# A three-stage kernel ordered by its own planner: the planner's durations, its margins and the priorities of the inverses are changed

## The chip, the cores and the metric

The kernel runs on one core of a Trainium2 chip. Five engines work beside each other, each through its own list of instructions and in the order of that list: TensorE (PE: matrix products, with PEld for loading weights), VectorE (DVE), ScalarE (ACT), GpSimd (POOL) and SyncE (SP), which here starts nearly all transfers. An instruction whose input is not there yet holds up everything behind it on its engine. The metric is the device time of one launch in microseconds (us); three runs of the kernel before gave 1203.41 us as the median, from 1199.62 to 1203.91.

## The reference

Three layers follow each other. The first is a recurrent attention with a state matrix, for 4 batches x 8 heads, 768 time steps and a head width of 48:

```python
for t in range(S):
    kt, vt, bt = (k_n[:, :, t], v[:, :, t], beta[:, :, t, None])
    y[:, :, t] = np.einsum('bhd,bhde->bhe', q[:, :, t], state)
    v_old = np.einsum('bhde,bhd->bhe', state, kt)
    state = state + bt[:, :, :, None] * np.einsum('bhd,bhe->bhde', kt, vt - v_old)
```

Its output, 3072 tokens x 384, goes through `h = x @ w_in` (384 x 2048), the curve `g` (0 up to h = -1, (h + 1)^2 / 4 up to h = 1, then h), and `g @ w_out`. The third layer scales each token by its root mean square and by `rms_g`, and computes `(silu(xn @ w_gate) * (xn @ w_val)) @ w_out` with a hidden width of 1536.

## The kernel before

**Attention.** Time is cut into 12 chunks of 64 steps. Within a chunk the recurrence becomes a triangular system, which is solved with its inverse. A unit `u` is one chunk of two batches (their 8 heads each, one batch on each half of the 128 partitions), so a chunk has two units. For units of two chunks together (`GRP`; the first two groups hold one chunk each) `inverse(g)` (L498) inverts the 32x32 triangles on POOL: 31 steps of a product `tmp` (L518) and an addition into `xi` (L524). Then ACT transposes the result into `nt` (L526), SP stores it, and for each unit POOL makes `wt` of it (`a_mz`, L545 and L546). `b_vn` (L600) scales the values in `kvb` on POOL. PE multiplies `wt` and `kvb` to `tr` (`b_tr`, L666), then `px`, `ds` and the transposed output `xps`.

**First network.** Block `j` is the 256 tokens of chunk `j`. For each of 16 slices `f` of the hidden width `m1(j, f)` (L747) does nine products into `hps`, two ACT instructions (L757, L758), a DVE maximum (L761), an ACT copy (L767) and a DVE subtraction (L769) that splits the result into two parts, and nine products into `acc`. A block ends with the root mean square (`m1_rms`, L808), whose result SP stores (L837).

**Weights.** They come as 64-bit numbers. `w_dec` (L245) loads a tile, and ACT and DVE decode it into two 32-bit parts. Tiles of the first network (`n == 1`, 32 of them) stay in SBUF; the 36 of the second (`n == 2`, DVE L280 to L285) are stored to HBM (`w2d`, L289) and loaded again later.

**Second network.** Its order is written out by hand; it begins after everything above and isn't touched by the change.

**What sets the order.** The stages of attention, weights and first network are Python generators, and `Flow` puts them in order while the program is built. A stage names its engine, a cost in us, what it needs, which buffers it takes and gives back, a priority and perhaps a `lag`. `Flow.start` (L80) reckons the earliest time at which a stage could run: its engine free, its needs done plus `lag` plus `HOP` if they come from another engine, its buffers free; a transfer (its cost is a pair) also waits for the transfers before it. `Flow.step` (L96) takes for each engine the stage that could start first (on PE: the least idle time, then the priority), and of these the earliest; it then adds the cost to the engine's reckoned time. So the order of each engine's list, which holds on the chip, comes from reckoned times. Beyond `RUSH` (45 us) a transfer is reckoned to land `LAND` after its bytes. Where PE is reckoned idle while the kernel starts, `spin` fills the gap with products nobody uses. `PG` (L842) gives the priority of each inverse group and of what prepares it; a lower number goes first.

Of the kernel before, what the change touches and what calls it, by code (L numbers as in the profile page):

```python
# [22 lines left out]
B, H, S, D = 4, 8, 768, 48  # L23
# [28 lines left out]
S = Stage  # L52


class Flow:
# [2 lines left out]

    HOP, ISSUE, FLY, LAND, RUSH = 0.4, 0.47, 0.65, 2.0, 45.0
    TILED = ("a_gram", "a_mw", "b_gs", "b_tr", "b_x", "b_ds")
    CHAIN = ("b_tr", "b_x", "b_xT")
    SWITCH, KEEP, STAY, AHEAD = 0.2, 10, 0, 0.9

    def __init__(self, **bufs):
# [13 lines left out]
    def start(self, p):  # L80
        key, st, i = p[1], p[3], p[4]
        t = self.free.get(st.eng, 0.0)
        for n in (*st.needs, (*key, i - 1)) if i else st.needs:
            if n not in self.done:
                return None
            e, x = self.done[n]
            t = max(t, x + st.lag + (0.0 if e == st.eng else self.HOP))
        if isinstance(st.cost, tuple):
            t = max(t, self.free.get("DMA", 0.0) - self.ISSUE - self.FLY - 0.7)
        for r in st.acq:  # L90
            if not self.toks[r]:
                return None
            t = max(t, self.toks[r][0] + self.HOP)
        return t

    def step(self):  # L96
        first = {}
        for p in self.live:
            st = p[3]
            if len(st.alt) > 1:  # L100
                st.eng, st.cost = min(st.alt, key=lambda a: max(self.free.get(a[0], 0.0), self.now) + a[1])
            t = self.start(p)
            if t is not None:
                e, k = p[3].eng, (t, p[0] + p[3].dp)
                if p[1][0] in self.CHAIN and p[1][1] < 2 and t < self.free.get(e, 0.0) + self.AHEAD:
                    k = (0.0, -500, t)
                elif e == "PE":
                    late = max(0.0, t - self.free["PE"] - 0.05)
                    k = (late, k[1] - ((self.KEEP if self.tiled else self.STAY) if (p[1][0] in self.TILED) == self.tiled else 0), t)
                if e not in first or k < first[e][0]:  # L110
                    first[e] = (k, p)
        if not first:
            return False
        t, p = min(((k[-1] if len(k) == 3 else k[0], p) for k, p in first.values()), key=lambda b: (b[0], b[1][0]))
        key, st, i = p[1], p[3], p[4]
        self.now, self.eng = t, st.eng
        if st.eng == "PE":
            self.idle(t - self.free["PE"])
            if (key[0] in self.TILED) != self.tiled:
                self.tiled = not self.tiled  # L120
                t += self.SWITCH
        for r in st.acq:
            self.toks[r].pop(0)
        if isinstance(st.cost, tuple):
            n, c = st.cost
            self.free[st.eng] = t + self.ISSUE * n
            end = max(self.free.get("DMA", 0.0), t + self.ISSUE + self.FLY) + c
            self.free["DMA"] = end
            end += self.LAND if t > self.RUSH else 0.9
        else:  # L130
            end = self.free[st.eng] = t + st.cost
        p[3], p[4] = next(p[2], None), i + 1
        self.done[(*key, i)] = self.done[key] = (st.eng, end)
        if p[3] is None:
            self.live.remove(p)
        else:
            del self.done[key]
        for r in st.rel:
            self.toks[r] = sorted(self.toks[r] + [end])
        return True  # L140
# [14 lines left out]
def kernel_body(  # L155
# [14 lines left out]
    stg = ctx.enter_context(tc.tile_pool(name="stg", bufs=4))  # L170
# [74 lines left out]
    def w_dec(n, f, i):  # L245
        if n == 2:
            needs = [("w_dec", 1, NF1 - 1, 1)]
        else:
            needs = [("a_gram", EARLY - 1)] if f + SK * i > 14 else []
        if n == 1:  # L250
            needs = needs + ([("inv0", 1 if f + SK * i < 9 else 19)] if f + SK * i >= 4 else [])
        me = ("w_dec", n, f, i)
        mem = "wp" if n == 1 and f + SK * i < 10 else "stg"
        yield S("SP", (1, 1.09) if n == 1 else (2, 2.18), needs, (mem,) * n)
        if mem == "wp":
            st = early([128, 2 * DM], "wst").bitcast(I64)
        else:
            st = stg.tile([128, DM], I64, name="wst", tag="wst")
        nc.sync.dma_start(out=st, in_=(w1 if n == 1 else w2)[f, :, DM * i:DM * i + DM])
        wu = st.bitcast(U32).rearrange("p (n t) -> p n t", t=2)  # L260
        wf = st.bitcast(F32).rearrange("p (n t) -> p n t", t=2)
        w0 = wu[:, :, 0]
        if n == 2:
            sv = stg.tile([128, 4 * DM], U16, name="wsv", tag="wst")
            nc.sync.dma_start(out=sv[:, 0:4 * DM - 2], in_=w2[f, :, DM * i:DM * i + DM].bitcast(U16)[:, 1:4 * DM - 1])
        yield S("ACT", 0.85, (), ("dec",))
        y = dcp.tile([128, DM], U32, name="dy", tag="dy")
        a = dac.pop(0)
        nc.scalar.activation(out=y.bitcast(F32), in_=wf[:, :, 1], func=ACTF.Copy, scale=2.0**-112)
        nc.scalar.activation(out=a.bitcast(F16).rearrange("p (n t) -> p n t", t=2)[:, :, 1], in_=wf[:, :, 1], func=ACTF.Copy, scale=2.0**-60)  # L270
        if n == 1:
            yield S("DVE", 1.5, (), ("wp",), (mem,))
            t = wp.tile([128, 2, DM], F32R, name="w", tag="w")
            yf = y
        else:
            yield S("DVE", 1.95, (), (), ("dec",))
            t = st.bitcast(F32R).rearrange("p (a b) -> p a b", a=2)
            yf = t[:, 0, :].bitcast(U32)
        hi, lo = t[:, 0, :], t[:, 1, :]
        nc.vector.scalar_tensor_tensor(out=yf, in0=y, scalar=3, in1=a, op0=ALU.logical_shift_left, op1=ALU.bitwise_or)  # L280
        nc.vector.tensor_scalar(out=a, in0=yf, scalar1=0xFF800000, scalar2=None, op0=ALU.bitwise_and)
        if n == 2:
            v = sv.bitcast(U32).rearrange("p (n t) -> p n t", t=2)[:, :, 0]
            nc.vector.tensor_scalar(out=v, in0=v, scalar1=0x1FFFFFF, scalar2=None, op0=ALU.bitwise_and)
            nc.vector.scalar_tensor_tensor(out=lo, in0=v, scalar=2.0**-36, in1=a.bitcast(F32), op0=ALU.mult, op1=ALU.mult)  # L285
            dac.append(a)
            yield S("SP", (1, 1.09), (), (), ("stg", "stg"))
            w2d[f, i] = dram.tile([128, 2, DM], F32, name=f"w2d{f}_{i}", tag=f"w2d{f}_{i}")
            nc.sync.dma_start(out=w2d[f, i], in_=t.bitcast(F32))  # L289
            return  # L290
        nc.vector.scalar_tensor_tensor(out=lo, in0=w0, scalar=2.0**-52, in1=a.bitcast(F32), op0=ALU.mult, op1=ALU.mult)
        dac.append(a)
        yield S("ACT", 0.41)
        nc.scalar.activation(out=hi, in_=y.bitcast(F32), func=ACTF.Copy)
        pre = f + SK * i <= PRE
        bank = "ea" if pre else "at"
        yield S("PE", 1.0, (), (bank,), ("dec",))
        if pre:
            fl.pre += 1
            ps = accp.tile([128, 512], F32, name="wlo", tag=f"acc{fl.pre % 2}")[:, 0:DM]  # L300
        else:
            ps = ap_.tile([128, DM], F32, name="wlo", tag="at")
        nc.tensor.matmul(out=ps, lhsT=ident, rhs=y.bitcast(F32), start=True, stop=False)
        nc.tensor.matmul(out=ps, lhsT=ineg_r, rhs=hi, start=False, stop=False)
        nc.tensor.matmul(out=ps, lhsT=ident_r, rhs=lo, start=False, stop=True)
        yield S("ACT", 0.45, (), (), (bank,), alt=[("DVE", 0.58)])
        if fl.eng == "ACT":
            nc.scalar.activation(out=lo, in_=ps, func=ACTF.Copy)
        else:
            nc.vector.tensor_copy(lo, ps)  # L310
        w1t[f, i] = t
# [433 lines left out]
    x2 = {}  # L745
# [62 lines left out]
    def m1_rms(j):  # L808
        yield S("ACT", 0.9, [("m1", j, NF1 - 1)], ("s",))
        t = x2[j]  # L810
# [22 lines left out]
        yield S("DVE", 1.3, (), (), ("w_",))  # L833
        for k in range(KD):
            nc.vector.scalar_tensor_tensor(out=t[:, k, :], in0=t[:, k, :], scalar=rg[:, k:k + 1], in1=ri, op0=ALU.mult, op1=ALU.mult)
        yield S("SP", (1, 1.09), (), (), ("x2",))
        nc.sync.dma_start(out=xn_d[j], in_=x2.pop(j))  # L837


    SK = 3  # L840
    PRE = 8
    PG = (-100, -50, -20, -10, 20, 50, 80)  # L842
    NW2 = 18
    fl = Flow(
        at=4, h=2, wp=34, stg=4, dec=ND, kk=2, ka=1, al=2, inv=1, tx=2, wt=2, z=2, kt=2, kvb=2, xs=2, xt=2,
# [14 lines left out]
    with tc.manual_schedule():  # L860
# [8 lines left out]
        fl.idle = spin  # L869
        fl.add(PG[0] + 6, inv0)  # L870
        for g, us in enumerate(GRP):
# [204 lines left out]
```

## Time and profile before

| | |
|---|---|
| median of 3 runs | 1203.41 us |
| the profiled execution's own time | 1204.66 us |
| its span | 1202.8 us |
| PE busy | 1119.7 us (93%) |
| DVE, ACT, POOL busy | 672.1, 576.2, 282.9 us |

The span runs from the first to the last instruction; the execution's own time is 1.9 us longer. Busy time is an average over parts with different limits, so the profile is read by stretches: the attention and the first network together last until about 748 us, the second network from there to the end. "Idle before" an instruction and what ended it say who waited for whom. The granted clock is the share of TensorE's full clock in a stretch.

### The profile page before, as it was taken

How to read it: one execution, taken by the hardware profiler on the slowest of the kernel's cores; microseconds unless marked ns; L12 is line 12 of the kernel's file. 1: busy time of each engine (PE TensorE's matmuls, PEld its weight loads, DVE VectorE, ACT ScalarE, POOL GpSimd, SP SyncE). 2: the span in 40 equal slices, each digit the busy share in tenths (PEclk: the TensorE clock that was granted, in tenths of full speed). 3: DMA queues.
4: the chain of work that ended last, by engine and by line, in shares of the span. 5: the costliest groups of instructions: out<-in, count | busy, mean ns of one | idle time of the engine just before them, and what ended most of it. 6: DMA issues, size and time to landing. Idle time of an engine off the chain costs nothing.

```text
span 1202.8 us, 27917 instructions
## 1 busy us (share of the span) xinstructions
PE 1119.7 (93%) x11526; PEld 1021.9 (85%) x11526; DVE 672.1 (56%) x1373; ACT 576.2 (48%) x1385; POOL 282.9 (24%) x479
## 2 busy tenths in 40 slices
PE   7877896897998999799999999999999999999998
PEld 6665686886998998799999999999888888888887
DVE  7968876867576768556465555543333333333333
ACT  4787765565856585555656566432222212122212
POOL 3283848557177108400100000000000000000000
PEclk9998998998988999899999999999999999999999
DMA  7986589584876585413212076010101001010000
GB/s 216 286 240 157 158 213 286 138 229 135 247 227 155 190 249 191 101 33 94 63 33 76 2 277 249 14 32 10 31 10 35 18 1 53 1 44 10 20 7 26
DMA packets 165902, 137.02 MB, mean 114 GB/s; under 512 B 115088, under 2 KB 127632, under 8 KB 165776
## 3 DMA queue, kind: packets, MB, share of 16 engines
q1 hardware_dynamic: 164960, 135.20, 37.8%
q8 instruction: 90, 1.47, 0.5%
q14 instruction: 36, 0.29, 0.1%
q10 hardware_dynamic: 816, 0.05, 0.0%
HBM read 100.88 MB, written 34.34 MB: 112 GB/s over the span
## 4 chain that ended last, share of the span: by engine, by line
PE 64%; POOL 15%; DVE 6%; DMA 5%; issue 4%; SPq 3%; ACT 3%; POOLq 0%; DVEq 0%; ACTq 0%
PE gv L725 8%; PE gv L724 8%; PE gv L726 8%; POOL xi L524 8%; PE acc L724 8%; PE acc L725 8%; PE acc L726 7%; POOL tmp L518 7%; PE hps L724 4%; PE hps L725 3%; PE hps L726 3%; SPq L509 2%; PE gs L611 2%; DMA nt<-scr_a 2%; DMA wst<-in_w 2%
## 5 line engine op out<-in xcount | busy, mean ns | idle before, releaser
L724 PE MATMUL acc<-g,w 128*128 128x256 f32 x648 | 190.5, 294 | 12.6 <-DVE x L806 6.9
L725 PE MATMUL acc<-g,w 128*128 128x256 f32 x648 | 187.0, 289 | 5.1 <-DVE g L769 5.1
L726 PE MATMUL acc<-g,w 128*128 128x256 f32 x648 | 185.8, 287 | 0.0
L724 PE MATMUL hps<-xh,w 128*128 128x256 f32 x576 | 168.1, 292 | 18.4 <-DVE w__4404 L761 6.1
L740 ACT ACTIVATE xh<-fix 128x512 fp32r<-128x512 f32 x60 | 37.9, 632 | 281.6 <-PE acc L726 275.7
L741 DVE TENSOR_TENSOR xl<-fix,xh 128x512 fp32r<-128x512 f32 x60 | 41.6, 694 | 228.9 <-ACT xh L740 228.9
L725 PE MATMUL hps<-xl,w 128*128 128x256 f32 x576 | 165.5, 287 | 0.0
L726 PE MATMUL hps<-xh,w 128*128 128x256 f32 x576 | 165.2, 287 | 0.0
L724 PE MATMUL gv<-fix,w 128*128 128x512 f32 x360 | 140.1, 389 | 0.0
L725 PE MATMUL gv<-fix,w 128*128 128x512 f32 x360 | 140.1, 389 | 0.0
L726 PE MATMUL gv<-fix,w 128*128 128x512 f32 x360 | 140.0, 389 | 0.0
L724 PEld LDWEIGHTS acc<-g,w 128*128 128x128 f32 x648 | 126.4, 195 | 15.4 <-DVE x L806 7.2
L725 PEld LDWEIGHTS acc<-g,w 128*128 128x128 f32 x648 | 126.7, 195 | 7.2 <-DVE g L769 7.0
L724 PEld LDWEIGHTS hps<-xh,w 128*128 128x128 f32 x576 | 113.0, 196 | 21.4 <-DVE w__4404 L761 6.4
L757 ACT ACTIVATE s<-hps 128x256 f32<-128x256 f32 x192 | 73.4, 382 | 111.8 <-PE hps L726 102.8
L726 PEld LDWEIGHTS acc<-g,w 128*128 128x128 f32 x648 | 126.6, 195 | 0.0
L518 POOL TENSOR_TENSOR tmp<-nt,xi 128x87 f32<-128x87 f32 (+21 forms) x186 | 102.4, 550 | 77.7 <-DMA nt<-scr_a 63.6
L524 POOL TENSOR_TENSOR xi<-xi,tmp 128x87 f32<-128x87 f32 (+21 forms) x186 | 111.0, 597 | 14.6
L725 PEld LDWEIGHTS hps<-xl,w 128*128 128x128 f32 x576 | 112.9, 196 | 0.0
L726 PEld LDWEIGHTS hps<-xh,w 128*128 128x128 f32 x576 | 112.8, 196 | 0.0
L758 ACT ACTIVATE s<-s,vhalf 128x256 f32<-128x256 f32 x192 | 97.9, 510 | 6.2
L726 PEld LDWEIGHTS gv<-fix,w 128*128 128x128 f32 x360 | 67.6, 188 | 14.1
(758 smaller groups left out, 2304.5 us busy)
## 6 DMA issues: line engine op xcount, KB each, us to landing
wst<-in_w SPq DMA_DIRECT2D x68, 384.0 KB
w2d<-wst SPq DMA_DIRECT2D x36, 384.0 KB
w<-w2d SPq DMA_DIRECT2D x36, 384.0 KB
wsv<-in_w SPq DMA_DIRECT2D x36, 383.5 KB
kvb<-in_kv SPq DMA_DIRECT2D x22, 384.0 KB
kt<-in_kqT SPq DMA_DIRECT2D x24, 256.0 KB
scr_a<-al SPq DMA_DIRECT2D x24, 256.0 KB
qs<-in_kqT SPq DMA_DIRECT2D x48, 128.0 KB
```

Of the source, the lines that this page charges most:

```text
L509: nc.sync.dma_start(out=nt[q:q + r], in_=scr_a[g][o:o + 32, :, :, 32 * e:32 * e + 32].rearrange("t u h s -> (u h) t s"),)
L518: nc.gpsimd.tensor_tensor(out=tv, in0=nt[:, m:32, j:m].to_broadcast([w, n, m]), in1=x[:, j:m, 0:m].to_broadcast([w, n, m]), op=ALU.mult,)
L524: nc.gpsimd.tensor_tensor(out=x[:, m:32, 0:m], in0=x[:, m:32, 0:m], in1=tv, op=ALU.add)
L611: nc.tensor.matmul(out=ps[half(b), h, 0:n], lhsT=kt[u][half(1 - b), 4 * k + h, :], rhs=qs[p][half(1 - b), b, 4 * k + h, 0:n], start=True, ...
L724: nc.tensor.matmul(out=out, lhsT=wh, rhs=xh, start=first, stop=False, skip_group_check=shared)
L725: nc.tensor.matmul(out=out, lhsT=wh, rhs=xl, start=False, stop=False, skip_group_check=shared)
L726: nc.tensor.matmul(out=out, lhsT=wl, rhs=xh, start=False, stop=last, skip_group_check=shared)
L740: nc.scalar.activation(out=hi, in_=src, func=ACTF.Copy)
L741: nc.vector.tensor_tensor(out=lo, in0=src, in1=hi.bitcast(F32), op=ALU.subtract)
L757: nc.scalar.activation(out=s, in_=ps, func=IDENTITY_SAT240, scale=240.0)
L758: nc.scalar.activation(out=s, in_=s, func=ACTF.Square, bias=vhalf, scale=1.0 / 480.0)
```

## The change

The change edits numbers that the planner reckons with, and no instruction. A table `SCALE` multiplies the reckoned cost of a stage by engine and name (22 entries; two are shown). `LAND` goes from 2.0 to 3.0 us. A transfer after `RUSH` is reckoned to start `MARGIN` = 1.0 us later than its data allow. The store of a decoded tile (L289) gets `lag=3.0`, the store of a block (L837) `lag=4.0`. In `PG` groups 2 to 6 get higher numbers, so that they and the loads and products that prepare them yield to more of the other work.

```diff
-    HOP, ISSUE, FLY, LAND, RUSH = 0.4, 0.47, 0.65, 2.0, 45.0
+    HOP, ISSUE, FLY, LAND, RUSH, MARGIN = 0.4, 0.47, 0.65, 3.0, 45.0, 1.0
...
+    SCALE = {
+        ("POOL", "inverse"): 1.2, ("POOL", "a_mz"): 1.3, ("POOL", "b_vn"): 1.15, ("PE", "a_mw"): 0.6, ("PE", "b_xT"): 0.6, ("PE", "b_x"): 0.85,
...
+        ("DVE", "w_dec"): 0.92, ("DVE", "m1"): 0.92, ("DVE", "m1_rms"): 0.75, ("DVE", "a_mw"): 1.1, ("DVE", "b_ds"): 1.1,
+    }
...
         if isinstance(st.cost, tuple):
-            t = max(t, self.free.get("DMA", 0.0) - self.ISSUE - self.FLY - 0.7)
+            t = max(t + self.MARGIN * (self.now > self.RUSH), self.free.get("DMA", 0.0) - self.ISSUE - self.FLY - 0.7)
...
-            end = self.free[st.eng] = t + st.cost
+            end = self.free[st.eng] = t + st.cost * self.SCALE.get((st.eng, key[0]), 1.0)
...
-            yield S("SP", (1, 1.09), (), (), ("stg", "stg"))
+            yield S("SP", (1, 1.09), (), (), ("stg", "stg"), lag=3.0)
...
-        yield S("SP", (1, 1.09), (), (), ("x2",))
+        yield S("SP", (1, 1.09), (), (), ("x2",), lag=4.0)
...
-    PG = (-100, -50, -20, -10, 20, 50, 80)
+    PG = (-100, -50, -5, 5, 34, 64, 94)
```

The lists of all engines change throughout. The numbers in names tell one buffer from another within one program; line numbers of the changed kernel are 6 higher from L66 on.

POOL at the fourth inverse (the group of chunks 6 and 7; `xi_3571`), kernel before: its last step, and what follows it. `wt_4315` and `wt_4336` are the two units of chunk 4, `kvb_4047` and `kvb_4075` their values.

```order
L518 TENSOR_TENSOR tmp_3640<-nt_3570,xi_3571 128x31
L524 TENSOR_TENSOR xi_3571<-xi_3571,tmp_3640 128x31
L545 TENSOR_TENSOR wt_4315<-tx_3566,c1_1113 128x8x32
L546 TENSOR_TENSOR wt_4315<-tx_3566,c0_1112 128x8x32
L545 TENSOR_TENSOR wt_4336<-tx_3590,c1_1113 128x8x32
L546 TENSOR_TENSOR wt_4336<-tx_3590,c0_1112 128x8x32
L600 TENSOR_TENSOR kvb_4047<-kvb_4047,n__1099 128x384
L600 TENSOR_TENSOR kvb_4075<-kvb_4075,n__1099 128x384
```

POOL at the same inverse in the changed kernel (now `xi_4001`), from the clearing of its buffer to its first step; `wt_4142` and `wt_4164` are chunk 4.

```order
L509 MEMSET xi_4001 128x1024
L510 AFFINE_SELECT xi_4001<-xi_4001 128x1024
L551 TENSOR_TENSOR wt_4142<-tx_4018,c1_1986 128x8x32
L552 TENSOR_TENSOR wt_4142<-tx_4018,c0_1985 128x8x32
L551 TENSOR_TENSOR wt_4164<-tx_4057,c1_1986 128x8x32
L552 TENSOR_TENSOR wt_4164<-tx_4057,c0_1985 128x8x32
L524 TENSOR_TENSOR tmp_4093<-nt_4000,xi_4001 128x31
L530 TENSOR_TENSOR xi_4001<-xi_4001,tmp_4093 128x31
```

The `wt` of chunk 4 moves from behind the inverse to ahead of it; its `kvb` stays behind. The `wt` of chunk 6 and of chunk 8 moves ahead of the fifth and the sixth inverse in the same way.

ACT at the transposition of the fourth inverse, kernel before. `g`, `s` and `hps` belong to the first network.

```order
L767 ACTIVATE g_4334<-w__4313 128x256
L767 ACTIVATE g_4348<-w__4332 128x256
L526 ACTIVATE nt_3570<-xi_3571 128x1024
L757 ACTIVATE s_4383<-hps_4354 128x256
L758 ACTIVATE s_4383<-s_4383,vhalf_91 128x256
```

ACT at the same place in the changed kernel:

```order
L763 ACTIVATE s_4861<-hps_4826 128x256
L764 ACTIVATE s_4861<-s_4861,vhalf_91 128x256
L763 ACTIVATE s_4867<-hps_4847 128x256
L764 ACTIVATE s_4867<-s_4867,vhalf_91 128x256
L532 ACTIVATE nt_4000<-xi_4001 128x1024
L568 ACTIVATE z_4917<-mg_4880 32x256 x2
L568 ACTIVATE z_4923<-mg_4900 32x256 x2
```

Ahead of this `nt` stand 42 slices of the first network (L757) before and 59 now. For the six inverses in turn these counts are 0, 11, 25, 42, 65, 96 before and 4, 19, 38, 59, 81, 117 now.

PE where chunk 4 meets `wt` and `kvb`, kernel before (`xh` is the first network's):

```order
L726 MATMUL hps_4680<-xh_4179,w_274 128x256
L666 MATMUL tr_4690<-kvb_4047,wt_4315 64x48 x16
L666 MATMUL tr_4714<-kvb_4075,wt_4336 64x48 x16
L557 MATMUL mg_4744<-tx_4451,g21_4453 32x32 x16
L424 MATMUL gk_4767<-ka_4660 64x64 x16
L679 MATMUL px_4787<-qs_353 64x48 x16
```

PE at the same place in the changed kernel:

```order
L732 MATMUL hps_4847<-xh_4159,w_1203 128x256
L831 MATMUL rps_4873<-sr_4658,ones_r_95 128x256
L832 MATMUL rps_4873<-sr_4658,ones_r_95 128x256
L563 MATMUL mg_4880<-tx_4373,g21_4375 32x32 x16
L563 MATMUL mg_4900<-tx_4406,g21_4408 32x32 x16
L672 MATMUL tr_4927<-kvb_4179,wt_4142 64x48 x16
L573 MATMUL mg_4880<-z_4917,g21_4375 32x32 x16
```

Ahead of the first `tr` of chunk 4 stand 50 groups of nine products into `hps` and 47 into `acc` before, 59 and 55 now. The transposed output of chunk 2 (`xps`) stood behind 46 groups of both kinds and now stands behind 58; block 2 begins behind 62 in both. The last decoding of a second-network tile stood ahead of the sixth `nt` on ACT; now 29 of the 36 do.

## Rows read from the trace of the kernel before

**Rows 1.** Stretches: us, busy of each engine (instructions), granted clock, DMA share, GB/s.

```profile
0.00:75.00 75.00, 60.71 (x1004) 51.12 (x1004) 63.59 (x152) 48.25 (x121) 31.97 (x66) 1.00 0.82 250
75.00:500.00 425.00, 359.95 (x5044) 339.12 (x5045) 300.68 (x616) 268.32 (x693) 238.19 (x396) 0.93 0.70 198
500.00:748.00 248.00, 248.00 (x3165) 244.50 (x3165) 138.73 (x319) 149.45 (x361) 12.72 (x18) 1.00 0.31 100
748.00:1203.00 455.00, 451.06 (x2317) 387.18 (x2315) 169.15 (x288) 110.13 (x213) 0.00 (x0) 1.00 0.06 21
```

**Rows 2.** Waits over the whole span: us in total, times, longest.

```profile
POOL wt L545 <- PE tr L666: 125.8, 5, 33.3
...
ACT nt L526 <- POOL xi L524: 23.9, 6, 8.3
...
DVE kvb L617 <- POOL kvb L600: 10.3, 1, 10.3
PE gs L611 <- issue: 9.7, 2, 8.0
```

**Rows 3.** Order of time on PE behind its three other long gaps: start, us, [idle before].

```profile
295.68 0.58 PE L724 MATMUL hps<-xh,w 128*128 128x256 f32 x1 [6.15 <-DVE w__4404 L761]
...
385.04 0.58 PE L724 MATMUL acc<-g,w 128*128 128x256 f32 x1 [4.91 <-DVE x L806]
...
494.24 0.58 PE L724 MATMUL acc<-g,w 128*128 128x256 f32 x1 [5.72 <-ACT g L767]
```

**Rows 4.** Order of time at the fourth inverse: POOL, ACT, DVE.

```profile
251.48 0.25 POOL L518 TENSOR_TENSOR tmp<-nt,xi 128x31 f32<-128x31 f32 x1 [17.44 <-DMA nt<-scr_a]
...
292.12 0.25 POOL L524 TENSOR_TENSOR xi<-xi,tmp 128x31 f32<-128x31 f32 x1
...
292.40 1.96 ACT L526 ACTIVATE nt<-xi 128x1024 f32<-128x1024 f32 x1 [8.31 <-POOL xi L524]
...
292.98 0.85 DVE L573 TENSOR_TENSOR wt<-mg,c 32x256 f32<-32x256 f32 x2 [5.19 <-POOL wt L545]
...
294.62 1.62 POOL L600 TENSOR_TENSOR kvb<-kvb,n__1099 128x384 f32<-128x384 f32 x2
```

**Rows 5.** Stretches right behind the four long gaps, columns as in Rows 1.

```profile
93.20:96.60 3.40, 3.40 (x33) 3.12 (x34) 3.23 (x8) 1.31 (x3) 0.00 (x0) 0.50 0.04 5
295.80:301.30 5.50, 5.50 (x26) 5.50 (x27) 3.88 (x12) 3.00 (x8) 0.44 (x1) 0.50 0.88 138
385.10:390.10 5.00, 5.00 (x23) 5.00 (x24) 2.75 (x7) 3.35 (x10) 1.62 (x2) 0.50 0.97 159
494.30:499.30 5.00, 4.51 (x19) 4.22 (x20) 2.47 (x5) 2.56 (x7) 1.64 (x2) 0.50 0.82 129
```

**Rows 6.** Order of time on PE: one group of nine products at full clock.

```profile
688.51 0.28 PE L724 MATMUL acc<-g,w 128*128 128x256 f32 x1
...
689.59 0.28 PE L724 MATMUL hps<-xh,w 128*128 128x256 f32 x1
```

**Rows 7.** Order of time: `tr` of chunks 3 and 4; POOL's `wt` of chunk 7.

```profile
248.83 2.07 PE L666 MATMUL tr<-kvb,wt 64*64 64x48 f32 x64
...
313.99 2.07 PE L666 MATMUL tr<-kvb,wt 64*64 64x48 f32 x64
...
417.27 0.62 POOL L545 TENSOR_TENSOR wt<-tx,c 128x256 f32<-128x256 f32 x1 [24.49 <-PE tr L666]
```

**Rows 8.** DVE by groups, 303 to 331 us (POOL nearly idle): count, busy, mean ns.

```profile
L285 DVE SCALAR_TENSOR_TENSOR wst<-wsv,da 128x384 fp32r<-128x384 uint32 x4 | 2.2, 559 | 0.1
...
L281 DVE TENSOR_SCALAR da<-wst 128x384 uint32<-128x384 uint32 x4 | 1.4, 360 | 0.1
```

**Rows 9.** The same groups from 255 to 290 us, beside the fourth inverse.

```profile
L285 DVE SCALAR_TENSOR_TENSOR wst<-wsv,da 128x384 fp32r<-128x384 uint32 x5 | 4.1, 811 | 0.2
...
L281 DVE TENSOR_SCALAR da<-wst 128x384 uint32<-128x384 uint32 x4 | 2.6, 658 | 0.1
```

**Rows 10.** The root mean square's DVE lines: ns min/median/max.

```profile
L832 DVE RECIPROCAL ri<-rt x12: 1739/1753/1754, 212.1 to 773.2; 128x256 f32<-128x256 f32 x12
...
L835 DVE SCALAR_TENSOR_TENSOR x<-x,rg,ri x36: 471/480/894, 214.0 to 775.7; 128x256 f32<-128x256 f32 x36
```

**Rows 11.** Span and mean granted clock of the core.

```profile
core 0: 1202.8 us, clock 0.976
```

More of the change, by code (lines that the diff above doesn't have):

```diff
@@ L55 @@
 class Flow:
-    HOP, ISSUE, FLY, LAND, RUSH = 0.4, 0.47, 0.65, 2.0, 45.0
+    HOP, ISSUE, FLY, LAND, RUSH, MARGIN = 0.4, 0.47, 0.65, 3.0, 45.0, 1.0
     TILED = ("a_gram", "a_mw", "b_gs", "b_tr", "b_x", "b_ds")
     CHAIN = ("b_tr", "b_x", "b_xT")
+    SCALE = {
+        ("POOL", "inverse"): 1.2, ("POOL", "a_mz"): 1.3, ("POOL", "b_vn"): 1.15, ("PE", "a_mw"): 0.6, ("PE", "b_xT"): 0.6, ("PE", "b_x"): 0.85,
+        ("PE", "a_gram"): 0.85, ("PE", "b_tr"): 0.85, ("ACT", "inverse"): 2.2, ("ACT", "a_mw"): 1.35, ("ACT", "b_tr"): 1.3,
+        ("ACT", "m1"): 1.12, ("ACT", "w_dec"): 1.13, ("ACT", "b_x"): 1.15, ("ACT", "b_xT"): 1.15, ("DVE", "b_gs"): 1.2, ("DVE", "a_coef"): 1.5,
+        ("DVE", "w_dec"): 0.92, ("DVE", "m1"): 0.92, ("DVE", "m1_rms"): 0.75, ("DVE", "a_mw"): 1.1, ("DVE", "b_ds"): 1.1,
+    }
     SWITCH, KEEP, STAY, AHEAD = 0.2, 10, 0, 0.9
```

## The prediction

> **What bounds the kernel now.** I read the stretches first. From 748 us on, in the second network, PE is busy for 451.06 of 455 us at full clock, and from 500 to 748 us for all of 248 [rows 1]. The change adds and removes no work there, so nothing is to be had behind 500 us. Up to 75 us PE is idle for 14.3 us (75 - 60.71), while the weights arrive and DVE is busy for 63.59. The stretch that decides is 75 to 500 us: PE busy 359.95 of 425, so 65.1 us idle, at a granted clock of 0.93 on average; the clock is 0.976 over the whole span [rows 11], so 28.9 us of PE's full speed (0.024 x 1202.8) are lost, and since the other stretches show 1.00, all of them here.
>
> Then the waits. ACT waited six times, 23.9 us in all, at `nt` for the last step of an inverse on POOL, and DVE once for 10.3 us at a `kvb` that POOL does behind the first inverse [rows 2]. PE has four long gaps: 8.0 us at `gs` [rows 2], and 6.15, 4.91 and 5.72 us, each put down to DVE or ACT [rows 3], 24.8 us together. The order of time at the fourth inverse shows what lies behind one of them: POOL takes the last step at 292.12, ACT stood still for 8.31 us in front of `nt`, DVE for 5.19 us in front of `wt`, which POOL makes behind the same inverse, and all slices of the first network were queued behind these two [rows 4]. PE's gap there ends at 295.68. The 4.91 and 5.72 us end at 385.04 and 494.24, just behind the fifth and sixth inverse. So POOL isn't busy enough to bound the kernel (238 of 425 us), but each time it finishes an inverse later than the lists of ACT, DVE and PE allow for, PE stops.
>
> A gap costs twice. Right behind these four the granted clock is 0.50, the lower of its two levels (1.2 instead of 2.4 GHz), while PE works nearly all the time: 3.4, 5.5, 5.0 and 5.0 us are in the rows [rows 5], 18.9 us, of which half, 9.4 us, is lost.
>
> **The change part by part.**
>
> *The reckoned time of an inverse.* The planner reckoned its 31 steps at 33.0 us: the sum over j of 0.36 + 0.004 x (31 - j)(j + 1) is 11.2 + 21.8. The fourth took 40.9 us on the chip (251.48 to 292.37) [rows 4]. The lag of 3.0 us at `nt` covers a part, so 40.9 - 33.0 - 3.0 = 4.9 us remained; the mean wait of ACT was 23.9 / 6 = 4.0 us [rows 2], which agrees. With the factor 1.2 the planner reckons 39.6 us, and with the lag 42.6, which leaves 1.7 us in hand. The lists say the same: ahead of the fourth `nt` ACT has 59 slices where it had 42. So this wait should go, and with it DVE's wait for the `wt` of chunk 4, which POOL now makes ahead of the inverse. What comes next at this place is the `kvb` of chunk 4, which stays behind the inverse, and for it PE's `tr`. That came at 313.99 [rows 7], 17.8 us behind the `kvb` (294.62 + 1.62) [rows 4]. Ahead of it stand 114 groups of nine products instead of 97; a group takes 1.08 us (688.51 to 689.59) [rows 6], so PE has 18.4 us more to do before it can be stopped there. The four gaps and what the clock lost behind them are 24.8 + 9.4 = 34.2 us. At best all of it goes; at worst none, if PE stops in other places for as long. I take three of the four, 26 us, nearer to the best end because both the planner's numbers and the lists point to it, and because the first (a `kvb` that stands behind the first inverse in both orders) goes only so far as DVE has more to do ahead of it.
>
> *POOL's new wait.* With `wt` ahead of the inverses four to six, POOL waits for the `tr` of the chunk before, which frees the buffer, and the inverse is queued behind. Before, POOL waited for `tr` 5 times, 125.8 us in all and at most 33.3 [rows 2], but with no inverse behind. For the fourth: `tr` of chunk 3 ended at 250.9 (248.83 + 2.07) [rows 7], four `wt` at 0.62 follow (as 417.27) [rows 7], so the first step would come at 253.4 instead of 251.48, 1.9 us later, and the `kvb` of chunk 4 too. The 17.8 us up to `tr` hide it. The results themselves have far more room: the fourth inverse, done at 292.37, was needed for the `wt` of chunk 7 at 417.27, and POOL even waited 24.49 us in front of that [rows 7]. So 0; without that cover it would be 1.9 us at the fourth and up to 33.3 at a later one.
>
> *The other gaps.* 65.1 - 24.8 = 40.3 us of small and middling gaps remain from 75 to 500 us. The margin of 1 us, the longer landing and the two lags on stores move transfers behind others that are ready, on SP's one list; the later group priorities push the loads and products of groups 2 to 6 back. All of it rearranges these gaps and none is aimed at one that I can name. I take 0, and as bounds half of them, 20 us less or 20 us more.
>
> *DVE is now reckoned too short.* The factors 0.75 and 0.92 lower costs that were already below the trace. The reciprocal takes 1.75 us, and the three products behind it 0.48 each, 1.44 [rows 10]; the planner reckoned 1.67 and 1.30, and now 1.25 and 0.98. The shortfall grows from 0.22 to 0.96 us, 0.74 more, in each of 11 blocks. If every one of them reaches PE that is 8 us, if none does 0; I take 4.
>
> Decoding depends on POOL. While POOL is nearly idle two of the four DVE instructions of a tile take 0.559 and 0.360 us [rows 8], beside the fourth inverse 0.811 and 0.658 [rows 9], 0.55 us more for the two. The Trainium skill, "SBUF — State Buffer", section "SBUF: two separate sides", says that VectorE and GpSimd share a pair of ports which one of them holds for a whole instruction, so that the other stops, and that this concerns VectorE instructions with two SBUF inputs or in a two-port mode. The trace agrees as far as DVE's durations go (0.559 to 0.811 us), and by that rule a plan in which DVE's cost doesn't depend on what POOL does is late beside every inverse; this is a rival below.
>
> *The sum.* -26 + 0 + 0 + 4 = -22 us. The profiled execution took 1204.66 us (its span of 1202.8 and 1.9 around it), 1.25 more than the median of 1203.41. 1204.66 - 22 = 1182.7; I say **1182 us**, nearer to the median's scale. Its own range is 1172 to 1194: all four gaps and no cost on DVE would give 1170.5, half of the 26 gained 1195.7.
>
> **The rivals.**
>
> *More goes than the four gaps.* If lists that come from better durations also take 10 of the 40.3 us, with all 34.2, the time is 1204.66 - 44 = 1160. For it: ACT was reckoned short as well, and its factors rise. Against: no single cause stands behind these gaps.
>
> *The waits move.* PE stops elsewhere for the 26 us that it no longer stops behind inverses: 1204 to 1208. For it: DVE is busy for 300.68 of 425 us [rows 1], so a late stage soon delays the next. Against: the four gaps have one cause, and that is corrected.
>
> *DVE beside POOL holds PE.* Of the 36 tiles some 17 would be decoded beside an inverse by the share of time (6 x 40.9 of 425 us, of 29 tiles ahead of the sixth `nt`). Each takes 1.1 us more than alone (twice the 0.55 of half its instructions). Until now the waits for POOL covered for that; with the cover gone 17 x 1.1 = 19 us return, and 8 us of the blocks' ends: -26 + 19 + 8 = +1, 1206.
>
> *The attention comes too late (the slower side).* In PE's list the transposed output of chunk 2 stood 16 groups ahead of block 2 (46 against 62), 17.3 us; now it stands 4 ahead, 4.3 us. Groups 2 and 3, on whose inverses chunks 2 to 5 rest, have priorities of -5 and 5 instead of -20 and -10. If the attention of blocks 2 and 3 is 20 us behind PE each, PE waits 2 x (20 - 4.3) = 31.4 us and loses 2 x 2.75 at half clock (5.5 us as in [rows 5]): 1182.7 + 37 = 1220. It gets slower than before from 4.3 + 8.3 us on at each of the two. For it: the cover is a quarter of what it was. Against: the inverses start when their input is there, and the reckoned landing is longer now.
>
> **How the numbers follow.** Forecast 0.45, more 0.15, waits move 0.12, DVE 0.12, attention too late 0.16. About 0.5% (6 us) is what a measurement of this kernel can tell from no change. Faster by more: 0.45 + 0.15 + 0.04 of the two in the middle = 0.64. Within: 0.16 of these and 0.01 of the last. Slower by more: 0.15 of the last and 0.04 of the middle ones, 0.19. The range from 1160 to 1212 leaves out a half of the case with more (0.08) and two thirds of the slowest (0.11).
>
> **What would show it.** Right: ACT's wait at `nt` for `xi` falls from 23.9 us to under 8; DVE's 10.3 at `kvb` to under 5; PE's busy time from 75 to 500 us at least 15 us nearer to full, with a clock above 0.93; POOL waits for `tr` directly ahead of the first steps of the later inverses, and PE doesn't stop at the `tr` of chunk 4. Wrong: these waits are gone and PE's idle time in the same stretch is still 60 us or more, then it moved; or PE stops at `px` or `xps` of chunks 2 and 3; or it stops at `hps` for DVE while a reciprocal or a decoding runs.

## The result, and the profile after

The changed kernel takes 1165.61 us (median of 4 runs, 1164.51 to 1167.10), the kernel before 1203.66 us beside it (4 runs): 0.969 of it, with a 95% interval of 0.967 to 0.972. That is 38 us faster, where 22 were forecast: inside the range of 1160 to 1212, outside the forecast's own range of 1172 to 1194, and next to the rival "more goes than the four gaps" (1160).

The stretches of the kernel after, with the columns of [rows 1]:

```profile
0.00:75.00 75.00, 63.48 (x1005) 55.55 (x1006) 58.38 (x138) 44.54 (x99) 32.23 (x65) 1.00 0.81 234
75.00:500.00 425.00, 389.71 (x5651) 370.07 (x5650) 310.28 (x648) 284.88 (x748) 232.14 (x383) 0.96 0.66 182
500.00:748.00 248.00, 248.00 (x2897) 244.62 (x2896) 152.55 (x347) 152.56 (x363) 20.18 (x33) 1.00 0.41 133
748.00:1165.00 417.00, 413.29 (x2002) 349.40 (x2000) 148.51 (x242) 92.35 (x176) 0.00 (x0) 1.00 0.07 21
```

and the answer to [rows 11]:

```profile
core 0: 1165.1 us, clock 0.984
```

PE's idle time from 75 to 500 us falls from 65.1 to 35.3 us (425 - 389.71), by 29.8; up to 75 us from 14.3 to 11.5, by 2.8. PE's busy time over the whole span falls by 5.2 us (1119.7 to 1114.5). That is mostly the clock: at the lower of its levels PE was busy for 45.9 us before and is for 34.7 now, summed over all stretches granted 0.50, and half of the difference is 5.6 us. (The clock's whole loss falls from 28.9 to 18.6 us, 0.016 x 1165.1, but part of that lay in idle time, where it costs nothing.) Among small shifts the other way are 22 more of the products that only fill gaps (160 `warm` for 138). 29.8 + 2.8 + 5.2 = 37.8, and the span is shorter by 37.7 (1202.8 to 1165.1). Behind 500 us PE is as full as it was.

The page's shares of the chain that ended last show the same thing in one line. The kernel before:

```profile
PE 64%; POOL 15%; DVE 6%; DMA 5%; issue 4%; SPq 3%; ACT 3%; POOLq 0%; DVEq 0%; ACTq 0%
```

The kernel after:

```profile
PE 81%; DVE 6%; POOL 4%; DMA 3%; issue 2%; ACT 2%; SPq 2%; POOLq 0%; DVEq 0%; ACTq 0%
```

The inverses on POOL have nearly left the chain. Of the waits in [rows 2], ACT's at `nt` is gone altogether (23.9 us before) and DVE's at `kvb` nearly. POOL's at `wt` is left, and PE's longest wait is now one that was 5.1 us in all before, for the subtraction `g` on DVE (us in total, times, longest):

```profile
POOL wt L551 <- PE tr L672: 111.9, 7, 32.5
...
PE acc L731 <- DVE g L775: 14.3, 7, 6.8
...
DVE kvb L623 <- POOL kvb L606: 1.2, 1, 1.2
```

Counted in the trace, PE had five gaps of 3 us and more between 75 and 700 us, 29.6 us together: the four of the prediction and one of 4.8 us on a transfer. Now there is one, of 6.8 us. Gaps of 1 to 3 us were 25.0 us together and are 21.5.

The fourth inverse in order of time, after (POOL, ACT, PE, POOL; start, us):

```profile
261.52 0.95 POOL L524 TENSOR_TENSOR tmp<-nt,xi 128x31 f32<-128x31 f32 x1 [2.62 <-DMA nt<-scr_a]
...
301.63 0.25 POOL L530 TENSOR_TENSOR xi<-xi,tmp 128x31 f32<-128x31 f32 x1
301.84 1.62 POOL L606 TENSOR_TENSOR kvb<-kvb,n__1973 128x384 f32<-128x384 f32 x2
...
305.87 1.99 ACT L532 ACTIVATE nt<-xi 128x1024 f32<-128x1024 f32 x1
...
309.88 1.94 PE L672 MATMUL tr<-kvb,wt 64*64 64x48 f32 x32 [0.35 <-DVE qs L627]
...
311.91 0.71 POOL L551 TENSOR_TENSOR wt<-tx,c 128x256 f32<-128x256 f32 x1 [8.45 <-PE tr L672]
```

Against [rows 4] the order is turned round: POOL takes the last step 9.5 us later than before (301.63 for 292.12), and nothing waits for it. ACT comes to `nt` 4 us behind it without having stood still, PE comes to `tr` 6.4 us behind the `kvb` (301.84 + 1.62), and `tr` of chunk 4 starts at 309.88 for 313.99 [rows 7], with 17 more groups of products done ahead of it. That is the first of the chunk's two units; the second, which stood directly behind it before, now comes at 315.82.

One thing is left at this place. PE's gaps ahead of `tr` are short (1.31, 0.64, 0.46 and 0.35 us), so the count of long gaps doesn't show them, but from 308.8 to 319.0 us the clock is at the lower of its two levels, its longest such stretch in this kernel (columns of [rows 1]):

```profile
308.80:319.00 10.20, 9.85 (x198) 9.30 (x192) 9.00 (x21) 3.88 (x10) 2.42 (x5) 0.50 0.87 194
```

### The profile page after: what moved, and what is told of

Its sections match the earlier page's. It is cut to its first block, busy times and chain, and to the rows that moved or that the text cites. A ratio compares the mean times of both kernels' runs of the same rounds, so it can differ in the third digit from the quotient of the medians.

```text
span 1165.1 us, 27941 instructions
## 1 busy us (share of the span) xinstructions
PE 1114.5 (96%) x11548; PEld 1019.6 (88%) x11548; DVE 669.7 (57%) x1374; ACT 574.3 (49%) x1384; POOL 284.5 (24%) x479
## 4 chain that ended last, share of the span: by engine, by line
PE 81%; DVE 6%; POOL 4%; DMA 3%; issue 2%; ACT 2%; SPq 2%; POOLq 0%; DVEq 0%; ACTq 0%
PE acc L730 10%; PE acc L731 9%; PE acc L732 9%; PE gv L732 8%; PE gv L731 8%; PE gv L730 8%; PE hps L730 5%; PE hps L732 5%; PE hps L731 5%; PE gs L617 3%; POOL xi L530 2%; POOL tmp L524 2%; PE px L685 2%; PE tr L672 2%; PE ds L699 1%
## 5 line engine op out<-in xcount | busy, mean ns | idle before, releaser
L731 PE MATMUL acc<-g,w 128*128 128x256 f32 x648 | 186.4, 288 | 14.3 <-DVE g L775 14.3
```

What stands on the lines that cost most here:

```text
L731: nc.tensor.matmul(out=out, lhsT=wh, rhs=xl, start=False, stop=False, skip_group_check=shared)
```

## The experiments

Every kernel was timed in rounds beside the kernel before; the ratio is to it, and the last column is ACT's wait at `nt` for POOL in the profile. The edits of kernels made from the kernel before leave out the lines that only make `MARGIN` and `SCALE` known (0.0 and an empty table where nothing else is said).

| kernel | median us | ratio (95%) | ACT at `nt`, us |
|---|---|---|---|
| before | 1202 to 1204 | | 23.9 |
| changed | 1165.6 | 0.969 (0.967 to 0.972) | none |
| inverses' factor alone | 1190.1 | 0.991 (0.989 to 0.992) | none |
| the whole table alone | 1174.3 | 0.977 (0.975 to 0.979) | none |
| priorities alone | 1204.6 | 1.002 (1.001 to 1.004) | 11.7 |
| margin, landing, lags alone | 1185.9 | 0.987 (0.985 to 0.988) | 6.3 |
| hop 0.42, kernel before | 1202.4 | 1.000 (0.998 to 1.001) | 19.3 |
| hop 0.42, changed kernel | 1161.7 | 0.967 (0.964 to 0.969) | none |
| lag 10 at `nt`, kernel before | 1200.2 | 0.998 (0.997 to 1.000) | 1.8 |
| changed without margin, landing, lags | 1178.0 | 0.979 (0.977 to 0.982) | none |
| ScalarE's factors alone | 1195.0 | 0.993 (0.992 to 0.995) | 28.0 |
| changed with the old priorities | 1160.8 | 0.967 (0.964 to 0.969) | none |
| changed, DVE's factors 1.1 | 1163.9 | 0.968 (0.966 to 0.971) | none |
| changed without the inverses' factor | 1161.8 | 0.967 (0.964 to 0.969) | 6.8 |

**One part alone: the inverses' factor.** The prediction's main step by itself.

```diff
+    SCALE = {('POOL', 'inverse'): 1.2}
```

> The kernel before with one number of the change: the planner reckons an inverse at 1.2 times its cost; nothing else. Ahead of the six transpositions ACT then has 3, 16, 32, 52, 70 and 97 slices (0, 11, 25, 42, 65, 96 before; 4, 19, 38, 59, 81, 117 in the changed kernel). Theory 'inverses': the gain of 38 us hangs on this wait, so most of it comes back, 1204 - 26 = 1178 (between 1170 and 1186), ACT's wait at nt falls under 6 us and the four long gaps of PE go. Rival 'all stages': the gain is spread over the table, the margins and the priorities, and this number alone gives at most a third, 1191 or more. Rival 'any other list': a small edit that shuffles the lists moves the time by 10 us either way.

It gave 12 us, not 26: 1190.1, a microsecond under the 1191 that "all stages" named and far from 1178. The wait went: no ACT wait at `nt` is left in the profile, and DVE's at `kvb` fell from 10.3 to 3.1 us. But PE's idle time from 75 to 500 us fell from 65.1 to 52.0 only, as the stretch shows (columns of [rows 1]). The two waits, DVE's and one of PE's new long ones, stand behind it:

```profile
75.00:500.00 425.00, 373.02 (x5289) 352.28 (x5286) 322.19 (x642) 280.77 (x717) 239.76 (x394) 0.96 0.70 200
```

```profile
PE gs L612 <- ACT rt L830: 5.9, 1, 5.9
...
DVE kvb L618 <- POOL kvb L601: 3.1, 3, 1.8
```

The four gaps of 24.8 us are gone as they were, and half of their time came back: PE has three gaps over 3 us here, 13.9 us together, one still at the end of the first inverse (4.95 us, up to 91.1) and two in new places (at 344 and 437 us), all put down to DVE or ACT.

**The table alone.** The kernel before with all 22 factors, nothing else.

```diff
+    SCALE = {
+        ("POOL", "inverse"): 1.2, ("POOL", "a_mz"): 1.3, ("POOL", "b_vn"): 1.15, ("PE", "a_mw"): 0.6, ("PE", "b_xT"): 0.6, ("PE", "b_x"): 0.85,
...
+    }
```

> The kernel before with the whole table of factors, without the margin, the longer landing, the lags of the two stores and the new priorities. Theory 'inverses': as with the inverses' factor alone, 1170 to 1186. Rival 'all stages': the table is the larger part of the change, 1175 to 1182, clearly faster than the inverses' factor alone (1191 or more).

28 us, so the other 21 factors gave 16 more. "All stages" holds: the table is clearly faster than its first factor, and its number (1175 to 1182) was missed by a microsecond.

**The priorities alone.**

```diff
-    PG = (-100, -50, -20, -10, 20, 50, 80)
+    PG = (-100, -50, -5, 5, 34, 64, 94)
```

> The kernel before with the new group priorities alone; costs and margins as before. Slices ahead of the six transpositions: 3, 11, 27, 49, 81, 110. Theory 'inverses': the inverses still end later than reckoned, so ACT still waits some 20 us at nt and PE keeps the gaps behind inverses; 1198 to 1208. Rival 'priorities': later groups alone put more slices ahead of the later inverses (81 for 65, 110 for 96) and hide the lateness, 1180 to 1190.

No gain, 2 us slower; the time is the one that "inverses" named. More slices stood ahead of the later inverses (110 instead of 96 at the sixth), ACT's wait fell to 11.7 us, and PE still had five long gaps. Among them was one of 9.0 us at 517 us, where the sixth inverse, now later, ended.

**Margin, landing and lags alone.** No table, old priorities.

```diff
-    HOP, ISSUE, FLY, LAND, RUSH = 0.4, 0.47, 0.65, 2.0, 45.0
+    HOP, ISSUE, FLY, LAND, RUSH, MARGIN = 0.4, 0.47, 0.65, 3.0, 45.0, 1.0
...
-            yield S("SP", (1, 1.09), (), (), ("stg", "stg"))
+            yield S("SP", (1, 1.09), (), (), ("stg", "stg"), lag=3.0)
...
-        yield S("SP", (1, 1.09), (), (), ("x2",))
+        yield S("SP", (1, 1.09), (), (), ("x2",), lag=4.0)
```

> The kernel before with the margin of 1 us, the landing of 3 us and the lags of the two stores alone. Theory 'inverses': a transfer rarely holds PE (6.2 us in all before), so 1195 to 1206, and ACT's wait at nt stays near 20 us. Rival 'transfers': SP stands some 70 us in front of the stores of decoded tiles, and what is queued behind it feeds everything; then 1180 to 1190.

16 us, more than the inverses' factor, and inside the band of "transfers", but not for its reason: SP's time in waits didn't fall (244.8 us before, 254.1 here, from 75 to 500 us). Three other things changed. First, ACT's wait at `nt` fell to 6.3 us without the inverse being reckoned longer, and of PE's five long gaps one was left, of 4.9 us. The plan puts a few more slices ahead of the first five transpositions (2, 13, 27, 46, 67, 96 for 0, 11, 25, 42, 65, 96), as a later reckoned landing of the inverse's input would make it. Second, ACT hardly waits for transfers any more. From 75 to 500 us in the kernel before:

```profile
ACT kk L375 <- DMA kk<-in_kv: 12.0, 4, 6.3
ACT dy L269 <- DMA wst<-in_w: 10.6, 10, 2.2
```

and in this one:

```profile
ACT dy L270 <- DMA wst<-in_w: 0.8, 1, 0.8
```

So the reckoned landing of transfers was too early as well, and margin and landing correct it. Third, tiles of the second network are decoded elsewhere. All 36 were done by 482 us before; here 27 were done by 500 us, and the rest up to 587, where PE is nearly full (243.8 of 248 us from 500 to 748) and DVE has room:

```profile
L286 DVE SCALAR_TENSOR_TENSOR wst<-wsv,da x36: 557/560/1069, 154.9 to 587.4; 128x384 fp32r<-128x384 uint32 x36
```

**A nudge that corrects nothing**, in the kernel before and in the changed one:

```diff
-    HOP, ISSUE, FLY, LAND, RUSH = 0.4, 0.47, 0.65, 2.0, 45.0
+    HOP, ISSUE, FLY, LAND, RUSH, MARGIN = 0.42, 0.47, 0.65, 2.0, 45.0, 0.0
...
-    HOP, ISSUE, FLY, LAND, RUSH, MARGIN = 0.4, 0.47, 0.65, 3.0, 45.0, 1.0
+    HOP, ISSUE, FLY, LAND, RUSH, MARGIN = 0.42, 0.47, 0.65, 3.0, 45.0, 1.0
```

> The kernel before with a change that corrects nothing: the planner reckons a hop between engines at 0.42 us instead of 0.40. All lists are shuffled (0, 11, 27, 43, 64, 94 slices ahead of the six transpositions). Theory 'durations' (the gain comes from reckoned times that are nearer to the chip's): the time stays within 6 us of 1202, and ACT still waits some 20 us at nt. Rival 'any other list': the time moves by 10 us or more, one way or the other, and the steps of 12 to 16 us of the earlier experiments say little.

> The same nudge (0.42 for 0.40 us a hop) in the changed kernel. Theory 'durations': within 6 us of 1166, since the reckoned durations are as good as before. Rival 'any other list': the 1166 us are a lucky list, and a shuffled one gives 1176 or more.

0.6 and 3.9 us. In these two tries shuffled lists moved the time by 4 us at most, so steps of 8 us and more are taken here as the edits' own, and differences of 4 us between variants of the changed kernel decide nothing. "Any other list", with its 10 us, has nothing for it.

**ACT's wait alone.**

```diff
-        yield S("ACT", 0.95, lag=3.0)
+        yield S("ACT", 0.95, lag=10.0)
```

> The kernel before with the lag at the transposition of an inverse 10 us instead of 3, so that ACT's list puts some 5 to 8 more slices ahead of it; the inverse's own reckoned time stays too short by 7 us, so the wt and kvb behind it on POOL are still expected too early by DVE and PE. If it is ACT's wait alone that costs, this gives what the inverses' factor gave, 1190. If DVE's and PE's waits for what POOL does behind an inverse cost as much, it gives half of that, 1194 to 1199.

2.8 us, less than either number: ACT's wait fell from 23.9 to 1.8 us and the time hardly moved. PE still has five long gaps, 28.7 us together (29.6 before). The waits now:

```profile
DVE kvb L618 <- POOL kvb L601: 20.6, 3, 11.7
...
PE gs L612 <- issue: 9.4, 1, 9.4
...
ACT nt L527 <- POOL xi L525: 1.8, 1, 1.8
```

DVE now stood 20.6 us for the `kvb` that POOL makes behind an inverse, at the first, second and fourth (10.3 before, at the first); PE's wait at `gs` was there before (8.0). So ACT's wait, the largest that the profile put down to the inverses, was worth next to nothing by itself: where it went, DVE waited behind the same inverses. ACT's list has nearly the same room here as with the inverses' factor alone (2, 15, 33, 50, 71, 99 slices ahead of the six transpositions for 3, 16, 32, 52, 70, 97), so some 9 of the 12 us there come from something other than ACT's room. The factor also moves back, in the plan, what DVE and PE do behind an inverse; that this is what pays is argued, not shown apart.

**The changed kernel without margin, landing and lags.**

The same three places set back, in the changed kernel.

```diff
-    HOP, ISSUE, FLY, LAND, RUSH, MARGIN = 0.4, 0.47, 0.65, 3.0, 45.0, 1.0
+    HOP, ISSUE, FLY, LAND, RUSH, MARGIN = 0.4, 0.47, 0.65, 2.0, 45.0, 0.0
...
-            yield S("SP", (1, 1.09), (), (), ("stg", "stg"), lag=3.0)
+            yield S("SP", (1, 1.09), (), (), ("stg", "stg"))
...
-        yield S("SP", (1, 1.09), (), (), ("x2",), lag=4.0)
+        yield S("SP", (1, 1.09), (), (), ("x2",))
```

> The changed kernel without the margin, the longer landing and the lags of the two stores; table and priorities stay. Alone those gave 16 us. If they still matter beside the table, 1175 to 1182; if the table already covers the same waits (both made ACT's wait at nt small), 1166 to 1170. With the table alone it was 1174, so this also says what the priorities do beside it.

12 us slower than the changed kernel, so they matter beside the table too. PE's idle time from 75 to 500 us is 46.1 us for 35.3 with them, though PE has one long gap in either kernel (8.1 us here, 6.8 there):

```profile
75.00:500.00 425.00, 378.85 (x5428) 357.90 (x5429) 327.52 (x675) 288.59 (x754) 222.49 (x362) 0.96 0.71 199
```

All 36 tiles were decoded before 500 us again (x36 by 498.8 us). ACT's waits for the same transfers are back, from 75 to 500 us:

```profile
ACT dy L275 <- DMA wst<-in_w: 14.3, 8, 3.8
...
ACT kk L381 <- DMA kk<-in_kv: 6.1, 4, 3.7
```

The three pairs with and without these edits say the same: 1202 and 1186 alone, 1178 and 1166 beside table and new priorities, 1174 and 1161 beside the table with the old ones; each time 12 to 16 us, each time with 27 or 28 instead of 36 tiles decoded by 500 us, and each time with ACT's waits for these two loads between 75 and 500 us down from 20 to 23 us to under 1. The runs don't part these two, nor the four numbers from each other.

**ScalarE's factors alone.**

```diff
+    SCALE = {('ACT', 'inverse'): 2.2, ('ACT', 'a_mw'): 1.35, ('ACT', 'b_tr'): 1.3, ('ACT', 'm1'): 1.12, ('ACT', 'w_dec'): 1.13, ('ACT', 'b_x'): 1.15, ('ACT', 'b_xT'): 1.15}
```

> The kernel before with ScalarE's seven factors of the table alone (inverse's transposition 2.2, a_mw 1.35, b_tr 1.3, b_x and b_xT 1.15, w_dec 1.13, m1 1.12). The inverses on POOL stay reckoned too short. The table gave 28 us and the inverses' factor 12 of them. Theory 'durations': each engine that is reckoned too short stands for itself, ACT was the one furthest off, and so most of the other 16 us come back here: 1188 to 1194. Rival 'only together': as long as the inverses end later than reckoned, ACT's better durations change nothing, 1198 or more.

8 us, one microsecond short of the expected band, with ACT's wait at `nt` still at 28.0 us. They don't need the inverses to be right.

**The changed kernel with the old priorities, and with DVE reckoned longer.**

```diff
-    PG = (-100, -50, -5, 5, 34, 64, 94)
+    PG = (-100, -50, -20, -10, 20, 50, 80)
```

> The changed kernel with the old group priorities (-20, -10, 20, 50, 80 for groups 2 to 6). Alone the new ones moved 1202 to 1204.6, and beside the table 1174 to 1178. If they do nothing for the time or a little against it, 1160 to 1168; if the chunks need them beside margin and lags, 1172 or more.

```diff
-        ("DVE", "w_dec"): 0.92, ("DVE", "m1"): 0.92, ("DVE", "m1_rms"): 0.75, ("DVE", "a_mw"): 1.1, ("DVE", "b_ds"): 1.1,
...
+    ... ('DVE', 'w_dec'): 1.1, ('DVE', 'm1'): 1.1, ('DVE', 'm1_rms'): 1.1, ('DVE', 'a_mw'): 1.1, ('DVE', 'b_ds'): 1.1}
```

> The changed kernel with VectorE's factors for w_dec, m1 and m1_rms at 1.1 instead of 0.92, 0.92 and 0.75, nearer to what the trace shows (reciprocal 1.84 us reckoned for 1.75). The prediction put the shortfall on DVE at 4 us, up to 8. If it costs that, 1158 to 1163; if DVE's lateness is hidden or a longer reckoned DVE spreads the work too thin, 1166 or more.

1160.8 and 1163.9 for 1165.6, with intervals that overlap its own. The first is the fastest median of all, 4.8 us below the changed kernel, hardly more than a nudge gives (3.9); the new priorities are worth nothing here, if they don't cost a little. The second is between its two bands and decides nothing.

**The changed kernel without the inverses' factor.** The test of the prediction's step from the other side.

```diff
-        ("POOL", "inverse"): 1.2, ...
```

> The changed kernel without the factor 1.2 for the steps of an inverse (3, 16, 33, 52, 82 and 113 slices ahead of the six transpositions). By themselves the factor gave 12 us, ScalarE's 8, the margin with landing and lags 16, the whole table 28, so the parts nearly add up. Theory 'each for itself': taking it out costs some 12 us again, 1174 to 1182, and ACT waits 15 to 20 us at nt. Rival 'the lag covers it': with the margin, the longer landing and the rest of the table the lists leave room enough for a late inverse, as with the margin alone, where ACT's wait fell to 6.3 us; then 1164 to 1170.

1161.8: nothing is lost, within the 4 us of a nudge. ACT waits three times at `nt`:

```profile
ACT nt L527 <- POOL xi L525: 6.8, 3, 3.1
```

"The lag covers it" holds, even below its band. The later reckoned landing, the margin and the other factors together leave about the room ahead of an inverse that its own factor leaves (3, 16, 33, 52, 82, 113 slices for 4, 19, 38, 59, 81, 117). So the parts don't add up in general. The table's 28 and the transfers' 16 us nearly do (44 against 42 for both together with the old priorities: 1202.8 - 1160.8), but the inverses' factor doesn't: 12 us alone, none beside the rest.

## Why the prediction was right, and which term was mis-sized

*What bounds the kernel, and where a gain can lie*: as said. Nearly all of it came from PE's idle time ahead of 500 us (29.8 and 2.8 us) and from the clock (some 5 us).

*The inverses end later than the lists allow for*: the wait was there and went, at `nt` and at `kvb`. **The size was the error.** The prediction took 26 of 34.2 us for the correction of the inverses' reckoned time. By itself it gave 12 us, and taken out of the changed kernel it cost nothing. The runs show two reasons: half of the time of PE's gaps came back in waits for DVE and ACT (inverses' factor alone); and room ahead of an inverse comes from the other edits as well (the last experiment, and the transfers alone, where one long gap of five was left). That the four gaps go all the same is right for the sum of the edits.

*The other gaps and the transfers, taken at 0*: this is the term that was missing. Margin, landing and lags gave 12 to 16 us, of the 20 that stood as the bound. The prediction had looked at what SP's list holds up, and not at ACT, which stood 22.6 us for two kinds of load from 75 to 500 us. In all three pairs two things go together: these waits go, and decoding moves out of the tight stretch. 9 tiles x (0.56 + 0.36 for two of four DVE instructions alone [rows 8], and ACT's two) are work that no longer stands in front of the slices there. Either can be the cause. The first is what the edits correct, a reckoned landing that was too early, and so an error of the same kind as the inverses'; the second is a side effect of theirs. Neither is shown by itself.

*ACT reckoned longer*, which the prediction named without a price in the rival "more goes": 8 us alone.

*POOL's new wait, 0*: right in its effect. At the fourth inverse it wasn't `tr` that held POOL: `tr` of chunk 3 ended at 249.7 (248.59 + 1.14), POOL then stood until 255.14 (5.90 us, put down to DVE) and 2.62 us for `nt`, and the inverse started 10.0 us later than before (261.52 for 251.48), not 1.9. Ahead of the fifth and the sixth POOL did wait for `tr`, 11.47 and 21.97 us, and they started 9.0 and 16.6 us later. ACT waited for none of the three.

*DVE reckoned too short, +4*: that it is too short shows in the trace below; what it costs can't be told from a nudge (1163.9 for 1165.6 with longer factors). The one long gap left is of this kind. PE stood 6.78 us up to 82.20 for a subtraction that DVE had queued behind tiles of the first network, decoded beside the first inverse, and behind six small instructions of the attention (79.60 to 81.74). The end of one tile, the last tile and the subtraction on DVE, and then PE:

```profile
76.25 0.91 DVE L297 SCALAR_TENSOR_TENSOR w<-wst,da 128x384 fp32r<-128x384 uint32 x1
77.08 0.97 DVE L286 SCALAR_TENSOR_TENSOR dy<-dy,da 128x384 uint32<-128x384 uint32 x1
78.09 0.70 DVE L287 TENSOR_SCALAR da<-dy 128x384 uint32<-128x384 uint32 x1
78.83 0.85 DVE L297 SCALAR_TENSOR_TENSOR w<-wst,da 128x384 fp32r<-128x384 uint32 x1
...
81.74 0.41 DVE L775 TENSOR_TENSOR g<-w__1065,g 128x256 fp32r<-128x256 f32 x1
```

```profile
82.20 0.58 PE L731 MATMUL acc<-g,w 128*128 128x256 f32 x1 [6.78 <-DVE g L775]
```

A tile takes 0.97 + 0.70 + 0.85 = 2.52 us here, and the planner reckons 1.5 x 0.92 = 1.38. So the rival "DVE beside POOL holds PE" names a real wait, once over 3 us, and not 19 us of it. Reckoning DVE longer didn't take it away (7.9 us in that kernel), which stays open.

*The attention comes too late*: it didn't. The first `tr` of chunk 4 came 4.1 us earlier with more done ahead of it, and PE had no long gap at `px` or `xps`.

*The sum*: its direction and its kind of cause, reckoned durations that were too short, were right. That the time lies inside the stated range is in part luck: the main term was more than twice what it gave alone, and the terms that made up for it, transfers and the other factors of the table, stood at 0. In size the rival "more goes than the four gaps" was the nearest; it had named ACT's factors, and not the transfers.

## What to carry to other kernels

Where a planner orders in-order engines, ask of each reckoned duration how far it is from the trace, and correct them together: one corrected number can move the wait to the next engine that is reckoned too short, and what it gives alone is not what it gives beside the others (12 us and none here). A wait that the profile puts down to one event can lie beside others at the same event; what it is worth is learnt by taking it away alone (here 23.9 us of waiting were worth 3). And slack on the reckoned landing of transfers can be worth as much as a corrected cost (12 to 16 us in three pairs here), whether because inputs have then landed when their reader comes to them or because work moves to a later stretch with room; a run that changes one of these without the other would tell.

## What the runs showed of the hardware

DVE's decoding got shorter by moving, not by changing: the same instruction (L285 before, L291 after) has a median of 720 ns before and 560 ns after, at the same minimum of 557. With no POOL instruction beside it, it takes 559 ns on average in both kernels and 561 at most; 16 of the 36 ran like that before and 19 after. The others took 854 and 809 ns on average.

```profile
L285 DVE SCALAR_TENSOR_TENSOR wst<-wsv,da x36: 557/720/1069, 146.5 to 482.3; 128x384 fp32r<-128x384 uint32 x36
```

```profile
L291 DVE SCALAR_TENSOR_TENSOR wst<-wsv,da x36: 557/560/1065, 146.3 to 585.5; 128x384 fp32r<-128x384 uint32 x36
```

Not every DVE instruction is longer beside POOL. In the kernel before the subtraction L769, whose inputs both lie in SBUF, takes 418 ns on average with POOL idle and 628 where POOL is busy for more than half of it; the maximum L761, with one input in PSUM, takes 420 and 414.
